# Linear attention into a snake MLP on one core: the first MLP group moved ahead of the second group's attention

## The chip, the cores and the metric

The kernel runs on one core of a Trainium2 chip, in one launch. The metric is the device time of a run in microseconds. The core's engines work side by side and wait for each other by semaphores: TensorE (PE, and PEld for its weight loads), VectorE (DVE), ScalarE (ACT), GpSimd (POOL) and SyncE (SP), which here issues transfers only.

## The reference

A causal linear attention with a decay per head, in blocks of 64, is followed by an MLP. Batch 4, 8 heads, 768 positions, head size 64; then 3072 tokens by 512 features, with 2048 hidden features.

```python
for b in range(nb):                       # blocks of 64 positions
    intra = einsum('bhic,bhjc->bhij', qb, kb) * Dmask      # lam**(i-j), causal
    intra = einsum('bhij,bhjd->bhid', intra, vb)
    inter = einsum('bhid,bhde->bhie', qb * lam_pow, kv_state)
    out[:, :, sl] = intra + inter
    kv_state = lam_block * kv_state + einsum('bhsd,bhse->bhde', kb * rev_pow, vb)
x = out.transpose(0, 2, 1, 3).reshape(B * S, H * D)
h = x @ w_in
s = sin(alpha * h)
g = h + s * s / (alpha + 1e-09)
y = g @ w_out
```

## The kernel before, in words

The work is cut into 24 units, `u` = 0 to 23. A unit is one batch, four heads and 256 positions, in two chunks of 128. Four units make a group of 512 tokens, so there are 6 groups, and the MLP runs by groups. The main loop walks through slots, `n` = 0 to 32.

**Loads.** `load(u)` (L68) issues the q, k and v of a unit, 256 KB each, on SyncE's queue, into a ring of 10 stage buffers. Before the loop the first 10 units are issued at once; in slot n unit n + 10 follows. The weights w_in and w_out come in four chunks each on GpSimd's queue (L135, L141), changed from fp32 to bf16 on the way.

**Scaling.** `scale(u)` (L149) makes three bf16 tiles: QL (q times a power of lam), KD (k divided by it) and VB (v). In the first group QL is made on VectorE and VB on ScalarE, otherwise all three on GpSimd. It is called two slots ahead.

**A slot of attention.** `transposes(u)` (L173) turns QL and KD on TensorE into one PSUM tile, pt, and ScalarE copies it to QT. `scores(u)` (L196) multiplies them into sp, which uses the same PSUM buffer as pt, and VectorE writes the masked ST from it. `kvmm(u)` (L218) makes the k-v products of the unit in the PSUM tile okv, and `kvupd(u)` (L233) updates the state: kvx on VectorE, kvbd and kvs on GpSimd, for each chunk. One slot later `intermm` (L261) and `outmm` (L275) put the attention output of the unit into okv (there is one okv, made anew for each slot), and `outev` (L291) has ScalarE copy it to xt. `slot(n)` (L302) puts these in order.

**The MLP.** `ffn1(g, f)` (L314) is one of 16 hidden blocks: four matmuls into hps (three PSUM buffers), Sin on ScalarE to s1, the square s2 on VectorE, and gall = s2 * r + hps on VectorE. `ffn2(g, m)` (L338) is one of four row blocks of the second layer: 16 matmuls into ops (one PSUM buffer), a copy to ob on ScalarE and a store on SyncE's queue.

**Order.** In slot n, four hidden blocks of group (n - 4) // 4 run between four blocks of four second-layer matmuls of group (n - 8) // 4; the transposes of the next unit stand behind the first of these (L390 to L395). So the first layer of group 0 runs in slots 4 to 7, beside the attention of group 1. TensorE's order is the written one (`manual_schedule`, L363). On the other engines a planner orders the instructions by its own priorities.

Of the kernel before, what the change touches and what calls it, by code (L numbers as in the profile page):

```python
# [9 lines left out]
ALU = mybir.AluOpType  # L10
ACTF = mybir.ActivationFunctionType
FP32 = mybir.dt.float32
BF16 = mybir.dt.bfloat16
PE = mybir.EngineType.PE


@with_exitstack
def kernel(
# [15 lines left out]
    C = 128  # L34
# [32 lines left out]

    def load(u):  # L68
        _, tp, b, _, hh = where(u)
        st = []  # L70
        for nm, src in (("q", q), ("k", k), ("v", v)):
            tl = stagep.tile([P, HH, 2, D], FP32, name=f"st_{nm}")
            nc.sync.dma_start(  # L73
                out=tl[:].rearrange("p h two e -> p h (two e)"),
                in_=src[b, hh * HH:(hh + 1) * HH, tp * W:(tp + 1) * W, :]
                .rearrange("h (p two) e -> p h (two e)", two=2))
            st.append(tl)
        stage[u] = st

    lam_bc = consts.tile([P, H], FP32, name="lam_bc")  # L80
    nc.sync.dma_start(out=lam_bc[:], in_=lam.partition_broadcast(P))
    alpha_r = consts.tile([NFC, P], FP32, name="alpha_r")
    nc.scalar.dma_start(out=alpha_r[:], in_=moe_alpha.rearrange("(f p) -> f p", p=P))
    for u in range(RING):
        load(u)
# [4 lines left out]
    for c in range(2):  # L90
# [11 lines left out]
    make_identity(nc, idf[:])  # L102
    cT = consts.tile([P, 1], FP32, name="cT")
    nc.vector.memset(cT[:], float(C))
    mask = consts.tile([P, 2, 2 * D], BF16, name="mask")
# [13 lines left out]
    lam_v = lam_bc[:].rearrange("p (hp two) -> p two hp", two=2)

    def make_lhp():
        for hd in range(2):
            sl = slice(hd * D, (hd + 1) * D)
            nc.gpsimd.tensor_tensor(out=LHP[sl, :], in0=lam_v[sl, hd, :],
                                    in1=cT[sl, :].to_broadcast([D, HP]), op=ALU.pow)
            nc.vector.tensor_copy(out=LBD[sl, :, hd], in_=LHP[sl, :])

# [173 lines left out]

    def slot(n, okv):  # L302
        if n < NU:
            scores(n)
        if 1 <= n <= NU:
            outmm(n - 1, okv)
            outev(n - 1, okv)
        if n < NU:
            kvmm(n, okv)
            kvupd(n, okv)  # L310

    gall = {}

    def ffn1(g, f):  # L314
        if f == 0:
# [3 lines left out]
        for c in range(NDC):  # L319
            def step(c=c):  # L320
                nc.tensor.matmul(out=hps[:], lhsT=w_in_sb[:, c, f * P:(f + 1) * P],  # L321
                                 rhs=xt[g][:, c].rearrange("p b c i -> p (b c i)"),
                                 start=(c == 0), stop=(c == NDC - 1))
            steps.append(step)

        def fin():
            s1 = mlps.tile([P, 512], BF16, name="s1")
            nc.scalar.activation(out=s1[:], in_=hps[:], func=ACTF.Sin,  # L328
                                 scale=alpha_sb[:, f:f + 1])
            s2 = mlps.tile([P, 512], BF16, name="s2")  # L330
            nc.vector.tensor_tensor(out=s2[:], in0=s1[:], in1=s1[:], op=ALU.mult)  # L331
            nc.vector.scalar_tensor_tensor(out=gall[g][:, f, :], in0=s2[:],  # L332
                                           scalar=r_sb[:, f:f + 1], in1=hps[:],
                                           op0=ALU.mult, op1=ALU.add)
# [26 lines left out]

    NM = NU + 8
    with tc.manual_schedule(engines={PE}):  # L363
        scale(0)
        run(transposes(0))
        scale(1)
        make_lhp()
        load_w_in(0)
        ap = ps.tile([P, NFC], FP32, name="ap", tag="ops", bufs=1)
        nc.tensor.transpose(out=ap[:], in_=alpha_r[:], identity=idf[:])  # L370
        nc.vector.tensor_copy(out=alpha_sb[:], in_=ap[:])
        nc.vector.reciprocal(out=r_sb[:], in_=alpha_sb[:])
        for n in range(NM + 1):
            g1, g2 = (n - 4) // 4, (n - 8) // 4
            A2 = A1 = None
            if n <= NU:
                slot(n, intermm(n - 1) if n >= 1 else new_okv())
            if n + 2 < NU:
                scale(n + 2)
            if n + RING < NU:  # L380
                load(n + RING)
            if n < 3:
                load_w_in(n + 1)
            elif n < 7:
                load_w_out(n - 3)
            T_ = transposes(n + 1) if n + 1 < NU else []
            A2 = ffn2(g2, n % 4) if 0 <= g2 < NG else []
            A1 = ([ffn1(g1, (n % 4) * 4 + i) for i in range(4)] if 0 <= g1 < NG
                  else [[] for i in range(4)])
            for i in range(4):  # L390
                run(A2[4 * i:4 * i + 4])
                if i == 0:
                    run(T_)
                run(A1[i])
            run(A2[16:])  # L395

# [29 lines left out]
```

## Time and profile before

| | us |
|---|---|
| median of 2 runs (lowest to highest) | 296.72 (296.6 to 296.84) |
| profiled run: time | 296.46 |
| profiled run: span from first to last instruction | 294.7 |
| TensorE busy in the span | 219.9 (75%) |
| VectorE busy | 157.9 (54%) |
| ScalarE busy | 121.6 (41%) |
| GpSimd busy | 106.9 (36%) |

The page's slices of the span, 40 of equal length (busy tenths of each engine, the granted TensorE clock in tenths, the DMA engines' busy share and what they moved), are read from left to right:

```profile
PE   0314518578578998899889988998899999999820
DVE  1812313866776666666666556655675666662000
POOL 6839957544654346434643344131000000000000
PEclk9999999987999999999999999999999999999995
DMA  7999999999943321000100010001000101111111
GB/s 189 261 267 253 237 215 272 287 290 291 290 122 78 103 68 35 19 26 31 36 23 24 31 38 21 24 30 38 20 24 29 38 28 35 41 39 39 51 51 39
```

A row of the timeline below gives the start, the duration, the engine and line, what is written from what, and in brackets how long the engine stood idle before it and what ended that. The lines of the chain in order of time give start, duration and the work. A matmul's duration is modelled and overlaps its neighbours, so the pace of matmuls is read from their starts or from the chain.

### The profile page before, as it was taken

What the parts mean: (1) busy time and instruction counts of PE and PEld (TensorE: products, weight loads), DVE (VectorE), ACT (ScalarE), POOL (GpSimd) and SP (SyncE); (2) the same over time, 40 slices, a digit from 0 to 9 for tenths busy, and PEclk for the clock granted to TensorE, in tenths of its full rate; (3) what the DMA queues carried; (4) which work ended last, traced back from release to release, by engine and by line L of the source; (5) the groups of instructions that cost most, each with busy time, mean ns of one, the idle gap of its engine ahead of it and who ended that gap; (6) DMA issues with size and microseconds to landing.
All of it is one profiled execution on the core that took longest, in us unless ns stands there. A gap on an engine that the chain in (4) does not pass through costs nothing.

```text
span 294.7 us, 5308 instructions
## 1 busy us (share of the span) xinstructions
PE 219.9 (75%) x2129; PEld 112.4 (38%) x2129; DVE 157.9 (54%) x293; ACT 121.6 (41%) x174; POOL 106.9 (36%) x160
## 2 busy tenths in 40 slices
PE   0314518578578998899889988998899999999820
PEld 0213414334244444444444444444444444444300
DVE  1812313866776666666666556655675666662000
ACT  2222214355444644454445444544454345451100
POOL 6839957544654346434643344131000000000000
PEclk9999999987999999999999999999999999999995
DMA  7999999999943321000100010001000101111111
GB/s 189 261 267 253 237 215 272 287 290 291 290 122 78 103 68 35 19 26 31 36 23 24 31 38 21 24 30 38 20 24 29 38 28 35 41 39 39 51 51 39
DMA packets 45560, 29.71 MB, mean 101 GB/s; under 512 B 1488, under 2 KB 42464, under 8 KB 45536
## 3 DMA queue, kind: packets, MB, share of 16 engines
q1 hardware_dynamic: 41280, 25.17, 31.2%
q0 software_dynamic: 4224, 4.19, 8.4%
q8 instruction: 16, 0.26, 0.4%
q14 instruction: 8, 0.07, 0.1%
q10 hardware_dynamic: 32, 0.01, 0.0%
HBM read 27.28 MB, written 6.29 MB: 114 GB/s over the span
## 4 chain that ended last, share of the span: by engine, by line
PE 55%; DVE 15%; SPq 8%; ACT 6%; DMA 5%; issue 5%; POOL 1%; ACTq 0%; POOLq 0%
PE hps L321 26%; PE ops L343 24%; SPq L73 8%; DVE ST L210 7%; DMA st_k<-in_k_dram 5%; PE pt L182 4%; DVE gall L332 4%; ACT ob L350 1%; ACT L328 0%; ACT xt L295 0%; PE okv L284 0%; DVE s_670 L331 0%; PE sp L203 0%; PE okv L268 0%; DVE s_1066 L331 0%
## 5 line engine op out<-in xcount | busy, mean ns | idle before, releaser
L321 PE MATMUL hps<-xt,w_in_sb 128*128 128x512 bf16 x384 | 101.5, 393 | 1.5 <-DVE gall L332 1.5
L343 PE MATMUL ops<-w_out_sb,gall 128*128 128x512 bf16 x384 | 96.7, 379 | 2.1 <-ACT ob L350 2.1
L321 PEld LDWEIGHTS <-w_in_sb 128*128 128x128 bf16 x384 | 38.0, 101 | 46.1 <-issue 8.1
L343 PEld LDWEIGHTS <-gall 128*128 128x128 bf16 x384 | 36.2, 98 | 44.6 <-issue 2.9
L188 ACT COPY QT<-pt 128x1024 bf16<-128x1024 bf16 x24 | 24.3, 1012 | 50.6 <-PE pt L182 50.6
L210 DVE TENSOR_TENSOR ST<-sp,mask 128x512 bf16<-128x512 f32 x48 | 32.4, 684 | 4.6 <-PE sp L203 4.6
L161 POOL TENSOR_TENSOR KD<-st_k,R 128x512 bf16<-128x512 f32 x24 | 24.9, 1040 | 16.5 <-DMA st_k<-in_k_dram 12.2
L182 PE MATMUL pt<-iden,QL 128*128 128x128 bf16 x96 | 10.8, 244 | 21.9 <-DVE ST L210 12.4
L168 POOL CAST VB<-st_v 128x512 bf16<-128x512 f32 x20 | 14.2, 711 | 33.8 <-PE okv L284 33.6
L295 ACT CAST xt<-okv 128x512 bf16<-128x512 f32 x24 | 14.1, 586 | 20.2 <-PE okv L284 18.4
L350 ACT COPY ob<-ops 128x512 f32<-128x512 f32 x24 | 14.1, 586 | 17.4 <-PE ops L343 17.4
L158 POOL TENSOR_TENSOR QL<-st_q,E 128x512 bf16<-128x512 f32 x20 | 20.8, 1042 | 0.0
L227 PE MATMUL okv<-VB,KD 64*64 64x64 bf16 x320 | 8.1, 207 | 15.8 <-ACT xt L295 15.8
L182 PEld LDWEIGHTS <-QL 128*128 128x128 bf16 x96 | 6.2, 106 | 29.9 <-DVE ST L210 20.2
L227 PEld LDWEIGHTS <-KD 64*64 64x64 bf16 x320 | 8.1, 118 | 18.7 <-issue 18.7
L203 PE MATMUL sp<-QT 64*64 64x128 bf16 x384 | 11.1, 241 | 2.0 <-ACT QT L188 2.0
L182 PE MATMUL pt<-iden,KD 128*128 128x128 bf16 x96 | 11.0, 246 | 0.6 <-POOL KD L161 0.6
L284 PE MATMUL okv<-ST,VB 64*64 64x128 bf16 x384 | 10.4, 232 | 0.0
L203 PEld LDWEIGHTS <-QT 64*64 64x64 bf16 x384 | 6.9, 116 | 4.9 <-ACT QT L188 2.1
L182 PEld LDWEIGHTS <-KD 128*128 128x128 bf16 x96 | 7.7, 112 | 0.8 <-POOL KD L161 0.8
L284 PEld LDWEIGHTS <-VB 64*64 64x64 bf16 x384 | 7.7, 118 | 0.1
L166 ACT CAST VB<-st_v 128x512 bf16<-128x512 f32 x4 | 2.5, 618 | 11.8 <-DMA st_v<-in_v_dram 11.8
(501 smaller groups left out, 273.2 us busy)
## 6 DMA issues: line engine op xcount, KB each, us to landing
st_q<-in_q_dram SPq DMA_DIRECT2D x24, 256.0 KB
st_k<-in_k_dram SPq DMA_DIRECT2D x24, 256.0 KB
st_v<-in_v_dram SPq DMA_DIRECT2D x24, 256.0 KB
out_dram<-ob SPq DMA_DIRECT2D x24, 256.0 KB
w_in_sb<-in_moe_w_in_dram POOLq DMA_DIRECT2D x4, 512.0 KB, 8.7
w_out_sb<-in_moe_w_out_dram POOLq DMA_DIRECT2D x4, 512.0 KB, 10.6
alpha_r<-in_moe_alpha_dram ACTq DMA_DIRECT2D x1, 8.0 KB
lam_bc<-in_lam_dram SPq DMA_DIRECT2D x1, 4.0 KB
```

Of the source, the lines that this page charges most:

```text
L73: nc.sync.dma_start(out=tl[:].rearrange("p h two e -> p h (two e)"), in_=src[b, hh * HH:(hh + 1) * HH, tp * W:(tp + 1) * W, :] .rearrange( ...
L158: eq.tensor_tensor(out=QL[:], in0=qs[:].rearrange("p h two e -> p two h e"), in1=E[:, :, hs].unsqueeze(3).to_broadcast([P, 2, HH, D]), op= ...
L161: nc.gpsimd.tensor_tensor(out=KD[:], in0=ks[:].rearrange("p h two e -> p two h e"), in1=R[:, :, hs].unsqueeze(3).to_broadcast([P, 2, HH, D ...
L182: nc.tensor.transpose(out=pt[:, j, hp, par, :], in_=src[:, par, 2 * hp:2 * hp + 2, :], identity=iden[:])
L188: nc.scalar.copy(out=QT[:], in_=pt[:])
L203: nc.tensor.matmul(out=sp[half[c], hd, par, hp, :], lhsT=QT[half[hd], 1, hp, par, half[c]], rhs=QT[half[hd], 0, hp, :, half[c]], start=Tru ...
L210: nc.vector.tensor_tensor(out=ST[:, hd], in0=sp[:, hd], in1=mask[:].unsqueeze(2).to_broadcast([P, 2, 2, P]), op=ALU.mult)
L227: nc.tensor.matmul(out=okv[half[hd], c, 2 * P + hp * D:2 * P + (hp + 1) * D], lhsT=KD[half[c], par, h, :], rhs=VB[half[c], par, h, :], sta ...
L284: nc.tensor.matmul(out=okv[half[hd], c, hp * P:(hp + 1) * P], lhsT=VB[half[c], par, 2 * hp + hd, :], rhs=ST[half[c], hd, par, hp, :], star ...
L321: nc.tensor.matmul(out=hps[:], lhsT=w_in_sb[:, c, f * P:(f + 1) * P], rhs=xt[g][:, c].rearrange("p b c i -> p (b c i)"), start=(c == 0), s ...
L343: nc.tensor.matmul(out=ops[:], lhsT=gall[g][:, f, m * P:(m + 1) * P], rhs=w_out_sb[:, f, :], start=(f == 0), stop=(f == NFC - 1))
L350: nc.scalar.copy(out=ob[:], in_=ops[:])
```

## The change

- Before the loop only units 0 to 3 are loaded. The load of unit 4, and with it the loads behind it on SyncE's queue (up to unit 13), waits for the last matmul of hidden block f = 9 of group 0.
- Slots 0 to 3 hold the attention of group 0 alone. Then all 16 hidden blocks of group 0 run in a row, with the square of the odd ones on GpSimd, and after them the scaling and the transposes of unit 4.
- In slots 4 to 6 the attention of group 1 runs beside second-layer row blocks 0 to 2 of group 0; slot 7 has no MLP work; row block 3 is spread over slots 8 to 11, beside the first layer of group 1. From slot 12 on the groups are as before.
- In a slot, the transposes of the next unit stand in the third round of MLP blocks instead of the first.
- In `slot`, kvmm comes ahead of the copy of okv to xt (outev).
- The order of GpSimd and SyncE is the written one too.
- w_in is issued in slots 0 and 1, two chunks each, behind the state update and the scaling; w_out after slot 3.
- lam to the power of 128 is made by repeated multiplication on VectorE instead of a power on GpSimd. A Sin of one element stands at the start of ScalarE's work.

```diff
+    GATE = 9
-    def load(u):
+    def load(u, after=None):
...
-            nc.sync.dma_start(
+            ld = nc.sync.dma_start(
...
+            if after is not None:
+                tc.add_manual_dep(ld.ins, after.ins.name, mybir.DependencyInfo(
+                    mybir.DependencyClass.Sync, mybir.DependencyReason.DATA))
+                after = None
...
+    nc.scalar.activation(out=warm[:], in_=warm[:], func=ACTF.Sin)
...
-    for u in range(RING):
+    for u in range(4):
         load(u)
...
+    LT = consts.tile([P, H], FP32, name="LT")
+    nc.vector.tensor_tensor(out=LT[:], in0=lam_bc[:], in1=lam_bc[:], op=ALU.mult)
+    for i in range(6):
+        nc.vector.tensor_tensor(out=LT[:], in0=LT[:], in1=LT[:], op=ALU.mult)
...
-    def slot(n, okv):
+    def slot(n):
+        okv = intermm(n - 1) if 1 <= n <= NU else new_okv()
         if n < NU:
             scores(n)
         if 1 <= n <= NU:
             outmm(n - 1, okv)
+        if n < NU:
+            kvmm(n, okv)
+        if 1 <= n <= NU:
             outev(n - 1, okv)
         if n < NU:
-            kvmm(n, okv)
             kvupd(n, okv)
...
-            nc.vector.tensor_tensor(out=s2[:], in0=s1[:], in1=s1[:], op=ALU.mult)
+            (sq or nc.vector).tensor_tensor(out=s2[:], in0=s1[:], in1=s1[:], op=ALU.mult)
...
+    def blocks(steps, k):
+
+        n = (len(steps) - 1) // k
+        bl = [steps[i * n:(i + 1) * n] for i in range(k)]
+        bl[-1] = bl[-1] + steps[-1:]
+        return bl
+
-    NM = NU + 8
-    with tc.manual_schedule(engines={PE}):
+    with tc.manual_schedule(engines={ET.PE, ET.Pool, ET.SP}):
         scale(0)
+        scale(1)
         run(transposes(0))
-        scale(1)
-        make_lhp()
-        load_w_in(0)
...
+        for n in range(4):
+            slot(n)
+            if n + 2 < 4:
                 scale(n + 2)
+            if n < 2:
+                load_w_in(2 * n)
+                load_w_in(2 * n + 1)
             if n < 3:
+                run(transposes(n + 1))
+        for j in range(4):
+            load_w_out(j)
+        okv = intermm(3)
+        outmm(3, okv)
+        outev(3, okv)
+        for f in range(NFC):
+            run(ffn1(0, f, nc.gpsimd if f % 2 else nc.vector))
+            if f == GATE:
+                load(4, after=f1mm[0, f])
+                for u in range(5, 4 + RING):
+                    load(u)
+        scale(4)
+        scale(5)
+        run(transposes(4))
+        NM = NU + 4
+        for n in range(4, NM):
+            if n < NU:
+                if n == 4:
+                    okv = new_okv()
+                    scores(4)
+                    kvmm(4, okv)
+                    kvupd(4, okv)
+                else:
+                    slot(n)
+                if n + 2 < NU:
+                    scale(n + 2)
+                if n + RING < NU:
+                    load(n + RING)
+            elif n == NU:
+                slot(n)
+            i = n % 4
+            g = n // 4
             T_ = transposes(n + 1) if n + 1 < NU else []
...
+            F1 = [ffn1(g - 1, 4 * i + j) for j in range(4)] if g >= 2 else []
+            if g == 1:
+                F2 = blocks(ffn2(0, i), 4) if i < 3 else []
+            elif g == 2:
                 if i == 0:
+                    late = blocks(ffn2(0, 3), 4)
+                F2 = [late[i]]
+            else:
+                F2 = blocks(ffn2(g - 2, i), 4)
+            nb = max(len(F1), len(F2), 3)
+            for j in range(nb):
+                if j < len(F2):
+                    run(F2[j])
+                if j == 2:
+                    run(T_)
+                if j < len(F1):
+                    run(F1[j])
+        for i in range(4):
+            run(ffn2(NG - 1, i))
```

## Rows read from the trace of the kernel before

**Rows 1.** Stretches: start and end, length, engines' busy time, granted clock, DMA.

```profile
0.00:48.10 48.10, 14.15 (x281) 10.99 (x282) 15.37 (x32) 10.96 (x14) 33.89 (x56) 1.00 1.12 239
48.10:81.22 33.12, 23.87 (x240) 11.55 (x239) 21.97 (x41) 17.30 (x23) 18.11 (x27) 0.90 1.11 290
81.22:236.92 155.70, 139.14 (x1400) 70.65 (x1398) 100.23 (x187) 76.48 (x111) 54.93 (x77) 1.00 0.13 40
236.92:281.80 44.88, 42.76 (x213) 19.18 (x211) 20.35 (x35) 16.29 (x25) 0.00 (x0) 1.00 0.12 40
```

**Rows 2.** The chain that ended last, shares of the span by line.

```profile
PE hps L321 26%; PE ops L343 24%; SPq L73 8%; DVE ST L210 7%; DMA st_k<-in_k_dram 5%; PE pt L182 4%; DVE gall L332 4%; ACT ob L350 1%; ACT L328 0%; ACT xt L295 0%; PE okv L284 0%; DVE s_670 L331 0%; PE sp L203 0%; PE okv L268 0%; DVE s_1066 L331 0%
```

**Rows 3.** Timeline of the startup, 0 to 50 us.

```profile
1.20 0.41 SPq L73 DMA_DIRECT2D st_q<-in_q_dram  x1
...
6.49 0.62 ACT L166 CAST VB<-st_v 128x512 bf16<-128x512 f32 x1 [4.03 <-DMA st_v<-in_v_dram]
...
7.60 0.95 POOL L137 DMA_DIRECT2D w_in_sb<-in_moe_w_in_dram  x1
...
13.49 0.64 PE L203 MATMUL sp<-QT 64*64 64x128 bf16 x16 [2.02 <-ACT QT L188]
...
15.39 0.28 DVE L245 COPY kvx<-okv 128x128 f32<-128x128 f32 x1
...
21.59 1.03 POOL L161 TENSOR_TENSOR KD<-st_k,R 128x512 bf16<-128x512 f32 x1 [3.66 <-DMA st_k<-in_k_dram]
...
24.03 0.37 PE L268 MATMUL okv<-QT,kvbd_256 128*128 128x128 bf16 x2 [7.47 <-DVE kvx L247]
...
29.07 0.37 PE L268 MATMUL okv<-QT,kvbd_349 128*128 128x128 bf16 x2 [1.58 <-DVE kvx L247]
...
48.10 4.27 PE L321 MATMUL hps<-xt,w_in_sb 128*128 128x512 bf16 x12
```

**Rows 4.** Timeline of a steady slot.

```profile
110.98 0.22 PE L268 MATMUL okv<-QT,kvbd_447 128*128 128x128 bf16 x1
...
112.62 0.32 PE L227 MATMUL okv<-VB,KD 64*64 64x64 bf16 x16 [0.69 <-ACT xt L295]
...
114.24 0.40 PE L182 MATMUL pt<-iden,QL 128*128 128x128 bf16 x4 [0.33 <-DVE ST L210]
...
120.74 0.22 PE L268 MATMUL okv<-QT,kvbd_539 128*128 128x128 bf16 x1
```

**Rows 5.** The chain in order of time: four MLP matmuls, start and duration.

```profile
115.72 0.86 PE ops L343 x4
```

**Rows 6.** Transfers by line: KB of each, median us from issue to landing.

```profile
w_in_sb<-in_moe_w_in_dram POOLq DMA_DIRECT2D x4, 512.0 KB, 8.7
```

**Rows 7.** Timeline of slots 4 to 7.

```profile
50.73 0.69 ACT L328 ACTIVATE s_668<-hps,alpha_sb 128x512 bf16<-128x512 f32 x1
...
51.45 0.92 DVE L331 TENSOR_TENSOR s_670<-s_668 128x512 bf16<-128x512 bf16 x1
...
52.40 0.75 DVE L332 SCALAR_TENSOR_TENSOR gall<-s_670,r_sb,hps 128x512 bf16<-128x512 bf16 x1
...
53.07 0.42 DVE L331 TENSOR_TENSOR s_679<-s_677 128x512 bf16<-128x512 bf16 x1
...
58.49 5.06 PE L321 MATMUL hps<-xt,w_in_sb 128*128 128x512 bf16 x16
...
72.75 0.28 PE L268 MATMUL okv<-QT,kvbd_891 128*128 128x128 bf16 x2
...
76.48 0.40 PE L182 MATMUL pt<-iden,QL 128*128 128x128 bf16 x4 [1.88 <-DVE ST L210]
...
81.22 0.28 PE L268 MATMUL okv<-QT,kvbd_1023 128*128 128x128 bf16 x2
```

**Rows 8.** Groups of instructions on GpSimd: count, busy us and mean ns, idle before.

```profile
L161 POOL TENSOR_TENSOR KD<-st_k,R 128x512 bf16<-128x512 f32 x24 | 24.9, 1040 | 16.5 <-DMA st_k<-in_k_dram 12.2 <-PE okv L227 3.4 <-POOL VB L168 0.9
```

**Rows 9.** Line 158 on VectorE: duration in ns, least, median and most.

```profile
L158 DVE TENSOR_TENSOR QL<-st_q,E x4: 628/678/3042, 8.1 to 13.1; 128x512 bf16<-128x512 f32 x4
```

More of the change, by code (lines that the diff above doesn't have):

```diff
@@ L13 @@
 BF16 = mybir.dt.bfloat16
-PE = mybir.EngineType.PE
+ET = mybir.EngineType
 @with_exitstack
@@ L76, in load @@
                 .rearrange("h (p two) e -> p h (two e)", two=2))
+            if after is not None:
+                tc.add_manual_dep(ld.ins, after.ins.name, mybir.DependencyInfo(
+                    mybir.DependencyClass.Sync, mybir.DependencyReason.DATA))
+                after = None
             st.append(tl)
         stage[u] = st
+    warm = consts.tile([1, 1], FP32, name="warm")
+    nc.vector.memset(warm[:], 0.0)
+    nc.scalar.activation(out=warm[:], in_=warm[:], func=ACTF.Sin)
     lam_bc = consts.tile([P, H], FP32, name="lam_bc")
@@ L102 @@
     make_identity(nc, idf[:])
-    cT = consts.tile([P, 1], FP32, name="cT")
-    nc.vector.memset(cT[:], float(C))
     mask = consts.tile([P, 2, 2 * D], BF16, name="mask")
@@ L118 @@
     nc.vector.memset(LBD[:], 0.0)
[L119 to L126, printed above, removed]
+    LT_v = LT[:].rearrange("p (hp two) -> p two hp", two=2)
+    for hd in range(2):
+        sl = slice(hd * D, (hd + 1) * D)
+        nc.vector.tensor_copy(out=LHP[sl, :], in_=LT_v[sl, hd, :])
+        nc.vector.tensor_copy(out=LBD[sl, :, hd], in_=LT_v[sl, hd, :])
     alpha_sb = consts.tile([P, NFC], FP32, name="alpha_sb")
@@ L306, in slot, with ffn1 @@
             outmm(n - 1, okv)
+        if n < NU:
+            kvmm(n, okv)
+        if 1 <= n <= NU:
             outev(n - 1, okv)
         if n < NU:
-            kvmm(n, okv)
             kvupd(n, okv)
     gall = {}
-    def ffn1(g, f):
+    f1mm = {}
+    def ffn1(g, f, sq=None):
         if f == 0:
@@ L320, in step @@
             def step(c=c):
-                nc.tensor.matmul(out=hps[:], lhsT=w_in_sb[:, c, f * P:(f + 1) * P],
+                f1mm[g, f] = nc.tensor.matmul(out=hps[:], lhsT=w_in_sb[:, c, f * P:(f + 1) * P],
                                  rhs=xt[g][:, c].rearrange("p b c i -> p (b c i)"),
@@ L372 @@
         nc.vector.reciprocal(out=r_sb[:], in_=alpha_sb[:])
[L373 to L378, printed above, removed]
+        for n in range(4):
+            slot(n)
+            if n + 2 < 4:
                 scale(n + 2)
-            if n + RING < NU:
-                load(n + RING)
+            if n < 2:
+                load_w_in(2 * n)
+                load_w_in(2 * n + 1)
@@ L382 @@
             if n < 3:
-                load_w_in(n + 1)
-            elif n < 7:
-                load_w_out(n - 3)
-            T_ = transposes(n + 1) if n + 1 < NU else []
[L387 to L391, printed above, removed]
-                if i == 0:
+                run(transposes(n + 1))
@@ L393 @@
                     run(T_)
-                run(A1[i])
-            run(A2[16:])
+                if j < len(F1):
+                    run(F1[j])
+        for i in range(4):
+            run(ffn2(NG - 1, i))
 _INS = ['q', 'k', 'v', 'lam', 'moe_w_in', 'moe_w_out', 'moe_alpha']
```

## The prediction, made before the changed kernel ran

> **What bounds the kernel now.** I read the stretches first, then the chain of waits, then the timeline inside each stretch. The stretches [rows 1] fall into four parts. In the first 48.10 us TensorE is busy for 14.15 us only, while the DMA engines are saturated at 239 GB/s and GpSimd is busy for 33.89 us. [...] From 81.22 to 236.92 (slots 8 to 23) it works 139.14 of 155.70 us at 1.00. From 236.92 to the end of the span, 57.8 us, it is busy 42.76 of 44.88 us and then leaves the last store to run out. The chain of waits [rows 2] agrees: MLP matmuls are half of the span, and of the rest the largest pieces are the load queue (8%), ST on VectorE (7%) and a k load (5%).
>
> The startup [rows 3] shows how loads get into the attention chain. Slot 0's scores run at 13.49 and its kvx is made by 15.39, but GpSimd, whose order a planner wrote, stands in front of a KD whose k tile has not landed (3.66 us of waiting, KD at 21.59). The state update of slot 0 is behind it, so slot 1 begins at 24.03 after 7.47 us of idle TensorE. Where no load is late, a slot takes 29.07 - 24.03 = 5.04 us. The first MLP matmul comes at 48.10.
>
> In the steady part [rows 4] a slot is 120.74 - 110.98 = 9.76 us. Four MLP matmuls take 0.86 us [rows 5], so the 32 of a slot take 6.91. Two idle times of TensorE are left: kvmm waits 0.69 us for the copy of xt, and the transposes wait 0.33 us for ST, whose PSUM buffer they share. So 9.76 - 6.91 - 0.69 - 0.33 = 1.83 us are attention's own matmuls.
>
> The profiled run's span of 294.7 lies 1.76 us under its time of 296.46, and the median is 0.26 above that time. I sum on the span and add 2.0.
>
> **Startup to the first MLP matmul: 30.2 instead of 48.10.** Only units 0 to 3 are loaded and GpSimd follows program order, so the KD of unit 4 no longer stands before slot 0's state update. Ahead of the first transposes GpSimd loses two LHP powers and one w_in issue (0.95 us, at 7.60 [rows 3]); the eight small LT multiplies that replace the powers go to VectorE, beside GpSimd's power for E. I take slot 0's scores at 11 (bounds 10 and the old 13.5). kvx comes 1.9 us later, as now; GpSimd's two products and the second kvx bring slot 1 to 11 + 3.7 = 14.7. Slots 1 and 2 take 5.04 each, slot 3 about 4 since no weight issue lies in it, and the last intermm, outmm and copy of xt 1.5 (an estimate from the 1.83 of all attention matmuls and a copy of about 0.6): 30.2. The two w_in issues now lie behind slot 0's update and the KD of unit 2, near 16.7 instead of 7.60, and the last two near 22. With 8.7 us from issue to landing [rows 6] the first two chunks are in near 26; the last two, for which the queue must bring 2 MB more, near 33. The first is needed at 30.2, the third at 41: hidden. The four w_out issues sit on GpSimd behind slot 3 (about 3 us, to 33), ahead of the first square there at 34; their 4 MB, read at the 290 GB/s of the second stretch [rows 1], land near 49 and are needed at 58. The Sin table load moves to the start, where ScalarE waits for data.
>
> **The first MLP group alone: 20.2 us.** [...] I take two f at 2 x 0.86 = 1.73 us each, 3.4 in all, then 14 limited by the three hps buffers. A buffer is filled (0.86), read by Sin (0.69), squared, and freed by gall (0.75) [rows 7]. With 0.3 of handing over (an estimate), an even f takes 0.86 + 0.69 + 0.42 + 0.75 + 0.3 = 3.0 us. An odd f has its square on GpSimd, which no row shows; the nearest row is KD, a 128x512 product too, at 1.04 [rows 8], giving 3.6. Over three buffers that is 1.1 us per f. VectorE's products of two SBUF tiles also vary while GpSimd is at work: QL took 0.63 us at best and 3.04 at worst [rows 9], and a square 0.92 instead of 0.42 [rows 7]. Half of one such delay per pair, 0.25, makes it 1.2. Bounds: 0.96 (VectorE's (0.42 + 0.75 + 0.75)/2) and 1.7 (the lower clock throughout). 3.4 + 14 x 1.2 = 20.2, so the group ends at 50.4.
>
> **The gate and the restart: 6.0 us of TensorE idle.** SyncE's load of unit 4 waits for the matmul of f = 9, at 30.2 + 3.4 + 8 x 1.2 = 43.2. Behind it on that queue are 29 more loads, and later the first stores, which nobody needs before slot 7. Unit 0's q, k and v were in 5.3 us after the first issue (from 1.20 to the cast at 6.49 [rows 3]); the same here gives 48.5. GpSimd, in order, has the square of f = 15 first, until 52.4, so the load is hidden; if w_out's packets double the 5.3, it is 53.8 and costs 1.4. Then QL and KD (2 x 1.04), transposes and the QT copy follow: scores of slot 4 at 56.4.
>
> **Slots 4 to 7: 22.6 us.** Slot 4 has 1.2 us of attention, 16 second-layer matmuls of which I put eight at the lower clock (3.45 + 1.73), and 0.46 of transposes: 6.9. Slots 5 and 6 have 3.45 + 1.83 = 5.3 of TensorE work, just over the 5.04 of a slot that GpSimd paces; slot 7 has no MLP: 5.04 less a weight issue, 4.3. With 0.8 for a colder start of slot 8 this is 22.6, and slot 8 begins at 79.0; now it begins at 81.22 [rows 7].
>
> **Slots 8 to 23: 133.1 instead of 155.7.** In slots 8 to 11 the work falls to 20 MLP matmuls, since three quarters of the second layer are done. TensorE then needs 4.32 + 1.83 = 6.15, and VectorE, whose work in a slot stays as it is, 100.23 / 16 = 6.3 [rows 1]. Today's slot 7, the same work less four matmuls, takes 81.22 - 72.75 = 8.5, with a 1.88 us wait of the transposes for ST in it [rows 7] and the 0.69 for xt; both go, since the transposes get two more blocks in front of them. 8.5 - 1.88 - 0.69 + 0.86 = 6.8; I take 7.2 for the slots in which VectorE's order gets in the way, 28.8 in all. In slots 12 to 22 both idle times go: kvmm stands before the copy, and the transposes behind five blocks (4.3 us) where now one block and 0.33 us are enough for ST. That is 11 x (9.76 - 1.02) = 96.1. Slot 23 has no transposes: 8.2. What is late next: QT's copy (1.01) has three blocks, 2.6 us, until the next scores; and kvx now stands behind the copy of xt in their PSUM bank, some 0.7 later, with 4 us to spare.
>
> **End: 57.8,** unchanged. Sum: 79.0 + 133.1 + 57.8 = 269.9, and 272 as a time.
>
> **Rivals.** *Cold start-up (8%).* TensorE stays at the lower clock until slot 8. For it: the granted clock was 0.90 between 48.10 and 81.22, where TensorE idled up to 1.88 us at a time, and 16 matmuls took 5.06 us [rows 1, 7]. Against: 0.90 is the mean of a stretch in which it rose again each time. All 16 f at 1.73 add 7.5, and slots 4 to 6 at 9.3 (16 x 0.43 + 2.4 of attention) add 10.4: 290. [...]
>
> *The wait changes place (10%).* The 0.69 us come back as a wait for kvx or the copy: 15 x 0.69 = 10.4 more, 282. [...]
>
> *Less in the way (17%).* The lone group at 0.96 per f (-3.4), slots 8 to 11 at TensorE's 6.15 (-4.2), no cold slot 8 (-0.8): 263.5. For it: VectorE was busy only 100.23 of 155.70 us [rows 1].
>
> *Planner's order stays (5%).* VectorE and ScalarE are still ordered by the planner, so the change does only part of what it says: if ST and kvx wait behind gall and the squares as in today's slot 7, slots 4 to 7 and 8 to 11 last 8.5 each at most, 34.0 instead of 22.6 for the first four, where VectorE has little else to do in three of them, so I count half of that, and 5.2 more for the others: 283.
>
> *Slower (3%).* The transposes moved so late that QT is not ready for the next scores. Place: slots 5 to 22, 18 of them. A slot loses whatever the copy exceeds 2.6 us; the change loses more than 2% from 1.7 us per slot on (30.8/18), that is, if the copy is done 4.3 us after the transposes. At 1.9 per slot it is 306. ScalarE, busy 76.48 of 155.70 us [rows 1], speaks against it.
>
> **How the numbers follow.** My sum has 57%, with its own range of 266 to 279 from the bounds (first scores +2.5/-1, the lone group -3.4/+7, w_out +1.4, slots 8 to 11 -4/+5, taken together rather than added). The range of 263 to 285 takes in 263.5 and 282, and leaves out the cold start and the slower case, 11%, and a little of the tails. A measurement here can tell about 2% from no change: under 290.8 is faster, over 302.7 slower. Faster: 57 + 10 + 17 + 5 and half of the cold case, 93%. The other half is no change, 4%. Slower 3%.
>
> **What would show it.** First MLP matmul near 30, a pace of 1.2 us per f and a longer idle time before slot 4's scores near 56; slot 8 near 79; slots of 7.2 and then 8.7 us, with no idle time before kvmm and the transposes. I am wrong if slot 8 starts past 95, if an idle time before scores names the QT copy, or if kvmm's 0.69 shows up under another name.

## The result, and the profile after

The changed kernel takes 268.25 us (median of 2 runs, 267.57 to 268.93) against 296.72: a ratio of 0.904 (95% interval 0.8941 to 0.914). The forecast was 272.0 with a range of 263 to 285, and faster. The profiled run took 267.57 us with a span of 265.8.

The first view is the table of stretches, cut where the prediction's steps end (start and end, length, each engine's busy time with its instructions, granted clock, DMA share, GB/s); it answers to [rows 1].

```profile
0.00:32.83 32.83, 11.15 (x234) 8.42 (x236) 13.17 (x38) 9.94 (x14) 18.85 (x39) 1.00 0.79 161
32.83:52.07 19.24, 16.27 (x62) 6.22 (x62) 12.53 (x21) 10.61 (x16) 9.86 (x11) 1.00 1.00 192
52.07:57.73 5.66, 1.22 (x9) 0.69 (x9) 2.38 (x4) 1.70 (x2) 4.80 (x6) 0.76 1.22 292
57.73:78.00 20.27, 17.41 (x259) 9.95 (x263) 7.11 (x16) 7.13 (x10) 15.86 (x26) 0.90 1.17 286
78.00:107.94 29.94, 24.69 (x315) 13.18 (x320) 21.63 (x44) 16.48 (x25) 18.29 (x28) 0.94 0.66 190
107.94:200.07 92.13, 91.45 (x947) 49.00 (x957) 73.19 (x128) 53.16 (x77) 44.24 (x58) 1.00 0.17 54
...
```

The first number of a line after its length is TensorE's busy time. From 107.94 on it works 91.45 of 92.13 us: nothing is left to wait for in slots 12 to 22. What is idle lies before that: most in the startup, then in slots 8 to 11 (24.69 of 29.94), the restart (52.07 to 57.73), the lone group (the first MLP group's first layer, which now runs by itself, 16.27 of 19.24) and slots 4 to 7 (17.41 of 20.27). Three of these stretches have a granted clock below 1.00. It is at its lower level, 0.50 in the profile, from 55.02 to about 61.9, in the restart and slot 4, and again from about 79 to 82, in slot 8.

A steady slot, in the timeline of TensorE, answers to [rows 4]:

```profile
116.31 0.22 PE L276 MATMUL okv<-QT,kvbd_805 128*128 128x128 bf16 x1
...
116.88 0.39 PE L292 MATMUL okv<-ST,VB 64*64 64x128 bf16 x16
117.10 0.29 PE L235 MATMUL okv<-VB,KD 64*64 64x64 bf16 x16
...
121.66 0.39 PE L190 MATMUL pt<-iden,QL 128*128 128x128 bf16 x4
...
124.69 0.22 PE L276 MATMUL okv<-QT,kvbd_917 128*128 128x128 bf16 x1
```

124.69 - 116.31 is 8.38 us, against 9.76. No row has an idle time in brackets: kvmm (L235) follows outmm (L292) after 0.22 us, and the transposes (L190) come behind five blocks.

The startup, in the timeline of all engines, answers to [rows 3]:

```profile
12.34 0.62 ACT L174 CAST VB<-st_v 128x512 bf16<-128x512 f32 x1 [2.10 <-DMA st_v<-in_v_dram]
...
13.92 0.64 PE L211 MATMUL sp<-QT 64*64 64x128 bf16 x16 [4.79 <-ACT QT L196]
...
17.62 0.37 PE L276 MATMUL okv<-QT,kvbd_228 128*128 128x128 bf16 x2 [0.62 <-DVE kvx L255]
```

Slot 1 begins at 17.62 instead of 24.03. But the scores of slot 0, at 13.92, are no earlier than before (13.49): ScalarE stands for 2.10 us in front of a cast whose v tile has not landed, and QT's copy, at 12.86, is behind it.

The restart, in the timelines of GpSimd (first two rows) and TensorE, answers to [rows 7, 8]:

```profile
52.92 1.04 POOL L344 TENSOR_TENSOR s_734<-s_732 128x512 bf16<-128x512 bf16 x1 [1.09 <-ACT s_732 L341]
53.92 1.04 POOL L166 TENSOR_TENSOR QL<-st_q,E 128x512 bf16<-128x512 f32 x1
...
55.02 0.61 PE L190 MATMUL pt<-iden,QL 128*128 128x128 bf16 x4 [2.95 <-POOL QL L166]
...
57.73 0.64 PE L211 MATMUL sp<-QT 64*64 64x128 bf16 x16 [1.10 <-ACT QT L196]
```

GpSimd makes the last square of the lone group first and then QL of unit 4, for which TensorE has stood since 52.07.

### The profile page after: what moved, and what is told of

The parts are those of the page before. It is cut to its first block, busy times and chain, and to the rows that moved or that the text cites. A ratio compares the mean times of both kernels' runs of the same rounds, so it can differ in the third digit from the quotient of the medians.

```text
span 265.8 us, 5296 instructions
## 1 busy us (share of the span) xinstructions
PE 212.6 (80%) x2104; PEld 110.6 (42%) x2129; DVE 156.7 (59%) x294; ACT 119.8 (45%) x174; POOL 112.5 (42%) x166
## 4 chain that ended last, share of the span: by engine, by line
PE 63%; POOL 13%; issue 6%; DVE 5%; ACT 4%; SPq 2%; DMA 2%; POOLq 0%; ACTq 0%
PE ops L356 30%; PE hps L334 24%; PE sp L211 3%; POOL KD L169 3%; PE pt L190 3%; POOL QL L166 2%; DMA st_v<-in_v_dram 2%; DVE gall L345 2%; SPq L74 2%; ACT QT L196 2%; PE okv L292 2%; PE okv L276 1%; POOL w_in_sb L145 1%; DVE ST L218 1%; DVE kvx L255 1%
## 5 line engine op out<-in xcount | busy, mean ns | idle before, releaser
L334 PE MATMUL hps<-xt,w_in_sb 128*128 128x512 bf16 x381 | 98.6, 384 | 7.8 <-DVE gall L345 6.8
L334 PEld LDWEIGHTS <-w_in_sb 128*128 128x128 bf16 x384 | 37.3, 99 | 53.3 <-issue 14.8
L166 POOL TENSOR_TENSOR QL<-st_q,E 128x512 bf16<-128x512 f32 x20 | 22.4, 1122 | 0.0
L190 PE MATMUL pt<-iden,QL 128*128 128x128 bf16 x96 | 10.4, 238 | 14.2 <-DVE QL L166 7.4
L190 PEld LDWEIGHTS <-QL 128*128 128x128 bf16 x96 | 7.3, 104 | 19.8 <-DVE QL L166 7.4
L176 POOL CAST VB<-st_v 128x512 bf16<-128x512 f32 x20 | 13.1, 656 | 0.0
L190 PE MATMUL pt<-iden,KD 128*128 128x128 bf16 x96 | 10.5, 239 | 0.7 <-POOL KD L169 0.7
L292 PE MATMUL okv<-ST,VB 64*64 64x128 bf16 x384 | 10.5, 232 | 0.0
L235 PE MATMUL okv<-VB,KD 64*64 64x64 bf16 x320 | 7.7, 205 | 0.0
L292 PEld LDWEIGHTS <-VB 64*64 64x64 bf16 x384 | 7.6, 117 | 0.3 <-issue 0.2
L190 PEld LDWEIGHTS <-KD 128*128 128x128 bf16 x96 | 7.1, 107 | 1.2 <-POOL KD L169 1.2
L235 PEld LDWEIGHTS <-KD 64*64 64x64 bf16 x320 | 6.4, 122 | 0.0
```

The lines of the kernel that those rows point to most:

```text
L166: eq.tensor_tensor(out=QL[:], in0=qs[:].rearrange("p h two e -> p two h e"), in1=E[:, :, hs].unsqueeze(3).to_broadcast([P, 2, HH, D]), op= ...
L190: nc.tensor.transpose(out=pt[:, j, hp, par, :], in_=src[:, par, 2 * hp:2 * hp + 2, :], identity=iden[:])
L235: nc.tensor.matmul(out=okv[half[hd], c, 2 * P + hp * D:2 * P + (hp + 1) * D], lhsT=KD[half[c], par, h, :], rhs=VB[half[c], par, h, :], sta ...
L292: nc.tensor.matmul(out=okv[half[hd], c, hp * P:(hp + 1) * P], lhsT=VB[half[c], par, 2 * hp + hd, :], rhs=ST[half[c], hd, par, hp, :], star ...
L334: f1mm[g, f] = nc.tensor.matmul(out=hps[:], lhsT=w_in_sb[:, c, f * P:(f + 1) * P], rhs=xt[g][:, c].rearrange("p b c i -> p (b c i)"), star ...
```

## The experiments

Each was timed in three rounds beside the kernel before; ratios are to that kernel, with their 95% interval. "After" is the changed kernel.

### The two edits in a slot

**One edit undone: the copy of xt again ahead of kvmm.**

```diff
+        if 1 <= n <= NU:
+            outev(n - 1, okv)
         if n < NU:
             kvmm(n, okv)
-        if 1 <= n <= NU:
-            outev(n - 1, okv)
```

> The changed kernel (268.25) with one thing undone: in a slot the copy of okv to xt stands ahead of kvmm again. Theory A, idle time read from starts: before the change kvmm began 1.09 us behind the first outmm matmul, after it 0.22, so the wait is worth 0.87 a slot. In the 12 slots 12 to 23, which TensorE paces, that is 10.4 us more, with up to 5 on top in slots 5 to 11: 279 to 284. Theory B, the idle time as printed (0.69): 8.3 more, 276 to 277. Theory C, the wait only changed its place: no more than 270.

Measured: 283.3 us (279.48 to 284.05), 0.957 (0.9554 to 0.9586). Timeline of TensorE, a steady slot:

```profile
118.29 0.39 PE L276 MATMUL okv<-QT,kvbd 128*128 128x128 bf16 x4
...
118.86 0.39 PE L292 MATMUL okv<-ST,VB 64*64 64x128 bf16 x16
119.94 0.32 PE L235 MATMUL okv<-VB,KD 64*64 64x64 bf16 x16 [0.69 <-ACT xt L303]
...
127.55 0.39 PE L276 MATMUL okv<-QT,kvbd 128*128 128x128 bf16 x4
```

The slot is 9.26 us. The bracket says 0.69, as in [rows 4], but kvmm begins 119.94 - 118.86 = 1.08 us behind outmm where after has 0.22: the wait is worth 0.86, and the slot is longer by 0.88. The printed idle time counts from the modelled end of the 16 small matmuls (118.86 + 0.39 = 119.25) and leaves a part out. The trace is of the quickest run, 279.48, and it accounts for that run: 1.1 us before slot 12 and 0.88 in each of slots 12 to 23 make up the 11.6 us by which its span is longer than that of after (277.4 and 265.8). The other runs took some 3 to 4 us more and have no trace, so where they lost that is not shown.

**The other edit undone: the transposes again behind the first block.**

```diff
-                if j == 2:
+                if j == 0:
                     run(T_)
```

> The changed kernel with one thing undone: the transposes of the next unit stand in the first round of MLP blocks again. Theory A: ST is ready 2.9 us after the scores begin, whatever TensorE does, so with kvmm early the transposes wait longer by just what kvmm gained: slots 12 to 22 go back to 9.76 us, 11 x 1.38 = 15 more, and some in slots 4 to 11: 283 to 288. Rival: the two edits add up, and this one is worth only its own 0.5 a slot, 5.5 more: 274.

Measured: 288.02 us, 0.9718 (0.9703 to 0.9732). Timeline of TensorE, a steady slot:

```profile
121.56 0.39 PE L276 MATMUL okv<-QT,kvbd 128*128 128x128 bf16 x4
121.88 0.42 PE L211 MATMUL sp<-QT 64*64 64x128 bf16 x16
...
122.58 1.04 PE L356 MATMUL ops<-w_out_sb,gall 128*128 128x512 bf16 x4
124.91 0.38 PE L190 MATMUL pt<-iden,QL 128*128 128x128 bf16 x4 [1.30 <-DVE ST L218]
...
131.50 0.39 PE L276 MATMUL okv<-QT,kvbd 128*128 128x128 bf16 x4
```

9.94 us: with the transposes early, what the earlier kvmm saves comes back in front of them, as 1.30 us for ST where [rows 4] has 0.33. ST is ready no earlier: the transposes begin 3.03 us after the scores here (121.88, 124.91) and 2.94 us in a slot of the kernel before (121.06, 124.00):

```profile
121.06 0.42 PE L203 MATMUL sp<-QT 64*64 64x128 bf16 x16
121.30 0.39 PE L284 MATMUL okv<-ST,VB 64*64 64x128 bf16 x16
122.39 0.32 PE L227 MATMUL okv<-VB,KD 64*64 64x64 bf16 x16 [0.69 <-ACT xt L295]
122.64 1.04 PE L343 MATMUL ops<-w_out_sb,gall 128*128 128x512 bf16 x4
124.00 0.40 PE L182 MATMUL pt<-iden,QL 128*128 128x128 bf16 x4 [0.33 <-DVE ST L210]
```

TensorE only reaches the wait sooner.

**Both undone.**

> The changed kernel with both orders within a slot undone, so that the new startup, the lone group and the in-order GpSimd and SyncE are left. Theory A: slots 12 to 22 at 9.76 us, 15 to 20 more than 268.25, and within 3 us of the run with the transposes alone undone: 283 to 289. Rival (the edits add up): the sum of the two increments.

Measured: 291.25 us, 0.9828 (0.9812 to 0.9844), a little above what was expected. This is the new startup alone: some 5 us, less than the 2% that can be told from no change here. The steady slots are those of the run before it, 9.94 us in slots 13 to 16 and 9.84 from slot 17 on, in both runs. So in a steady slot kvmm alone gives nothing, the later transposes alone about 0.6 (9.84 to 9.26) and both together 1.46 (to 8.38). The edits do not add: the time that the first saves in front of kvmm is lost in front of the transposes until the second moves these. Slot 23 shows it from the other side. It has no transposes, and there the earlier kvmm pays by itself: 8.81 us in this run, 7.93 in the one before. The rest of the 3.2 us between the two runs lies mostly in slot 8 (9.79 and 7.52), where TensorE was at about half pace in this run (the first four second-layer matmuls take 1.89 us, at 82.69) and not in the other (1.04, at 80.59).

**The two edits alone, in the kernel before.** There kvmm moves ahead of the copy and the transposes behind the fifth block:

```diff
             outmm(n - 1, okv)
-            outev(n - 1, okv)
         if n < NU:
             kvmm(n, okv)
+        if 1 <= n <= NU:
+            outev(n - 1, okv)
+        if n < NU:
             kvupd(n, okv)
...
-                if i == 0:
+                if i == 2:
                     run(T_)
```

> The kernel before (296.72) with only the two orders within a slot changed: kvmm ahead of the copy to xt, transposes behind the third block of second-layer matmuls. Theory A: slots 8 to 22 at 8.38 instead of 9.76 take off 20.8, slot 23 0.9, slots 4 to 7 another 4 to 8: 267 to 271, that is as fast as the whole change. Rival: the startup, the lone group and the orders of GpSimd and SyncE bring a third or more of the gain, and this run stays above 276.

Measured: 267.85 us (266.09 to 268.5), 0.9028 (0.8993 to 0.9062): as fast as the whole change. Two of its stretches, slot 4 and slots 8 to 11, and a row of its timeline in slot 4:

```profile
40.54:53.81 13.27, 7.18 (x74) 3.62 (x75) 4.56 (x10) 5.10 (x7) 7.81 (x12) 0.88 1.13 258
...
74.47:107.87 33.40, 33.40 (x368) 17.71 (x366) 25.65 (x50) 19.35 (x28) 19.72 (x28) 1.00 0.55 144
```

```profile
52.15 1.86 PE L323 MATMUL hps<-xt,w_in_sb 128*128 128x512 bf16 x4 [6.00 <-DVE gall L334]
```

Slot 12 begins at 107.87, in the changed kernel at 107.94, with the same work done. So the rearranged startup, as it stands, is worth nothing beside the slot edits: its first MLP matmul comes 9.4 us earlier (32.83, here 42.22), and it gives that back in the restart and in slots 8 to 11, which here run without any idle time (33.40 of 33.40). Nor is the old startup at its best. The 6.00 us of waiting in slot 4 are the fault of [rows 3] once more: in the chain of waits a k load ends at 48.55, and behind it follow on GpSimd the KD that it feeds (48.69), kvbd and kvs, and on VectorE kvx (50.69), a square and the gall that TensorE waits for.

### The parts of the new startup

**No gate:** the load of unit 4 no longer waits for f = 9 (`load(4, after=f1mm[0, f])` becomes `load(4)`).

> The changed kernel without the gate: the loads of units 4 to 13 follow those of unit 3 at once. Theory A: the gate costs nothing (GpSimd came to unit 4's scaling only when its last square was done, at 53.92) and protects little, since the w_in chunks are needed 10 us after they land: 267 to 270. Rival, the purpose of the gate: the loads delay w_in by half of its 6.6 us to landing or more, and the first MLP matmul comes 4 us or more later: 272 or more.

Measured: 267.87 us, 0.9046 (0.9021 to 0.907), no different from after. The median landing of a w_in chunk went from 6.6 to 10.9 us and of w_out from 8.9 to 14.4, but slot 12 begins at 107.98. Holding the loads back does what it says to the transfers and nothing that the time shows. The trace has a small effect under it: slot 5 begins 1.0 us later than in after (65.06 and 64.05), and slot 8 is 1.0 us shorter (6.74 and 7.73), since TensorE was at half clock there in after (0.50 from about 79 to 82) and at full pace here: the slot's second-layer matmuls, of which the traces have three, take 1.49 us in after and 0.81 here.

**GpSimd in the planner's order** (`engines={ET.PE, ET.SP}`).

> The changed kernel with GpSimd ordered by the planner again. It puts the KDs of units 2 and 3 ahead of slot 0's state update, w_in earlier, and unit 4's scaling among the squares of the lone group. Theory A (my prediction's step): a KD ahead of the state update makes the first slots wait for loads, the startup loses 2 us or more, and a square waits behind the scaling for unit 4's load: 270 to 274. Rival: with four units loaded first no load is late any more, so the order does not matter: 267 to 269.

Measured: 273.53 us, 0.924 (0.9214 to 0.9267). Scores of slot 0 move to 16.25, QL of unit 4 goes between the squares, at 49.75, and yet slot 8 begins at 80.91 and slot 12 at 112.83. The written order on GpSimd is worth some 5 us.

**ScalarE in written order too** (`ET.Activation` added).

> The changed kernel with ScalarE in written order too; it differs in the startup alone, where the first QT copy no longer stands behind the cast of unit 2's v. Theory A: in the changed kernel scores of slot 0 came at 13.92 and not at 11 because that copy waited for this load; in order it runs behind unit 1's cast (9.62 + 0.62), scores at 11.3, and the 2.6 us carry through the startup: 265 to 266.5. Rival: weights or loads are next in line, and nothing is left of it by slot 4: 268.

Measured: 266.76 us, 0.9025 (0.8986 to 0.9063), just above the expected range. The scores of slot 0 come at 11.04, the predicted 11, but of these 2.9 us slot 1 keeps 0.9 (16.69 against 17.62). A row of TensorE's timeline says why:

```profile
15.03 0.61 PE L190 MATMUL pt<-iden,QL 128*128 128x128 bf16 x4 [3.13 <-DVE ST L218]
```

Now VectorE, still planned, stands with ST behind unit 3's QL, which begins at 13.08 after 1.65 us of waiting for its load. The same fault, one engine on. By slot 5 nothing is left of the 0.9 (64.10 against 64.05), as the rival had it. Slot 12 is 0.9 earlier (107.03) only because slot 8, at full pace (0.81 us for the same three), takes 6.74 us here, against 7.73 in after, where the clock was at 0.50 for some 3 us of it.

**VectorE and ScalarE in written order** (`ET.DVE` as well).

> The changed kernel with VectorE and ScalarE in written order too. With ScalarE alone in order, scores of slot 0 came at 11.04, but VectorE stood in front of unit 3's QL, whose load was late, and ST came 2 us later. Theory A: both engines in order remove both waits; slot 1 begins at 14.7 instead of 17.62, as my sum had it, and the 2.9 us last to the end: 264.5 to 266. Rival: w_in or the loads of units 2 and 3 are next, and no more than the 1.5 us of ScalarE alone is left: 266.5 to 268.

Measured: 266.09 us, 0.8986 (0.8957 to 0.9014), between the two ranges. Slot 1 begins at 14.94 (predicted 14.7), 2.7 us earlier than in after, and the first MLP matmul at 30.92 (30.2), 1.9 earlier. At slot 8 1.4 us are left (76.59). Slot 12 is 2.4 us earlier (105.54), but 1.0 of that is slot 8, which ran at half clock in after (0.50) and at full pace here (6.74 us, and 0.81 for the same three matmuls). So about half of the gain lasts. Slots 9 to 11 still take 7.40 us each: the planner's order on VectorE was not what held them.

### The lone MLP group and the restart

**All squares on VectorE:** `run(ffn1(0, f, nc.gpsimd if f % 2 else nc.vector))` becomes `run(ffn1(0, f))`.

> The changed kernel with all squares of the lone group on VectorE. Theory A: the group then runs at VectorE's pace, 0.42 + 0.75 = 1.17 us per f, hardly slower than the 19.65 us that it takes now, and GpSimd is free to scale unit 4 as soon as its loads land, near 50, instead of 53.92, so scores of slot 4 come 2 to 4 us earlier: 264 to 267. Rival: eight squares more on VectorE cost 3.4 us, and the load is no earlier: 270 to 272.

Measured: 260.8 us (260.07 to 262.77), 0.8819 (0.8772 to 0.8867), better than expected. The timeline of all engines, 48 to 59 us:

```profile
48.07 1.04 POOL L166 TENSOR_TENSOR QL<-st_q,E 128x512 bf16<-128x512 f32 x1 [12.97 <-DMA st_q<-in_q_dram]
48.16 1.23 DVE L344 TENSOR_TENSOR s<-s 128x512 bf16<-128x512 bf16 x1
...
54.11 0.42 PE L211 MATMUL sp<-QT 64*64 64x128 bf16 x16 [1.23 <-ACT QT L196]
```

The lone group itself is no faster (its last matmul ends at 52.27, against 52.07). But GpSimd, free, makes QL of unit 4 as soon as its load is there, 48.07 instead of 53.92, so slot 4's scores come 3.6 us earlier. Slot 5 comes 5.6 earlier (58.49, and 64.05 in after). The other 2 us are the clock: from 57.73 to about 61.9 TensorE works at half pace, which makes 2.1 us of work out of 4.2. Two tables of stretches, first of after, then of this kernel (granted clock third from the right):

```profile
55.00:56.00 1.00, 0.61 (x4) 0.34 (x4) 0.00 (x0) 0.00 (x0) 1.00 (x2) 0.51 1.22 290
...
60.00:62.00 2.00, 2.00 (x6) 0.71 (x5) 0.29 (x1) 0.00 (x0) 1.59 (x4) 0.54 1.22 290
```

```profile
52.00:54.00 2.00, 0.88 (x10) 0.53 (x8) 1.97 (x4) 1.53 (x2) 2.00 (x3) 1.00 1.17 302
54.00:56.00 2.00, 1.84 (x38) 1.13 (x40) 1.96 (x5) 0.06 (x1) 0.52 (x1) 1.00 1.20 289
```

In after TensorE stands from 52.07 to 55.02, and restarts at a clock of 0.51; it is back at 1.00 by 62 (62 to 64), and six matmuls take the 2 us from 60. Here, with idle times of 1.23 us at most, it stays at 1.00. Slot 8 adds 1.0 us: 7.73 in after, at half clock (0.50) from about 79 to 82, and 6.74 here. That last microsecond can't be put down to the restart, since without the gate or with ScalarE in order the restart is at half pace too (0.64 us for slot 4's 16 score matmuls, 0.42 here) and slot 8 takes 6.74 all the same.

**Squares on GpSimd for odd f below 8 only** (`... if f % 2 and f < 8 else nc.vector`), to part the restart from the pace of the group.

> The changed kernel with the odd squares on GpSimd for f below 8 alone, so half of them on GpSimd and the late ones on VectorE. It tells what made all squares on VectorE 7.4 us faster. Theory A: the restart. [...] Rival: the pace of the lone group, in which eight squares of 1.04 us on GpSimd stand between hps and gall: half of the gain, 264 to 265.

Measured: 262.25 us, 0.8847 (0.8825 to 0.887): 6.0 of the 7.4 us, more than the rival's half, though half of the GpSimd squares are left. What costs is GpSimd being busy when unit 4 lands, and what follows from it, rather than its slower square. TensorE is at full pace in slot 4, behind a wait of 1.24 us (0.42 us for the 16 score matmuls, at 54.45), and at half pace in slot 8 from 73 to about 76.5 (0.64 us for the same, at 73.00; the clock's mean from 58 to 78 is 0.91), behind waits of 1.14 and 0.97 us in slot 7. The kernel with all squares on VectorE has the same two waits in slot 7, and there slot 8 is at full pace (0.42, at 72.65; the clock is 1.00 from 58 to 78). What decides this is not shown.

### Going further

**Squares on VectorE, and kvs ahead of kvbd on GpSimd:** the second chunk's kvx needs kvs alone, so the product that makes kvs is issued before the one for kvbd.

```diff
             bd = kvp.tile(...)
-            nc.gpsimd.tensor_tensor(out=bd[:], ...)
             ...
                 nc.gpsimd.tensor_tensor(out=prev[:], ...)
+            nc.gpsimd.tensor_tensor(out=bd[:], ...)
```

> All squares on VectorE (260.8), and in the state update kvs is made ahead of kvbd on GpSimd. Theory A: in slots 8 to 11 TensorE waits 1.40 us for gall because VectorE, in its order, stands in front of the second kvx, which waits for kvs behind kvbd; with kvs 0.6 us earlier each of these slots is 0.6 shorter, and each of the first slots 0.3 (kvbd is then the last to come): 256.5 to 259. Rival: VectorE's work sets these slots, the wait only moves to another square: 260 to 261.

Measured: 257.38 us (256.77 to 258.6), 0.8697 (0.8664 to 0.8729), the best of all. The total was expected, the place was not: slots 9 to 11 still take 7.40 us each, as in after. One of them in TensorE's timeline:

```profile
79.35 0.38 PE L190 MATMUL pt<-iden,QL 128*128 128x128 bf16 x4 [0.54 <-DVE ST L218]
...
81.57 1.02 PE L334 MATMUL hps<-xt,w_in_sb 128*128 128x512 bf16 x4 [0.75 <-DVE gall L345]
```

The 1.40 us wait for gall of after has split in two, both for VectorE. VectorE is now at work for 20.33 of the 22.19 us of these three slots (17.80 of 22.21 in after): there the rival was right. Against the kernel with all squares on VectorE (260.8), 1.6 us are gained in the startup, 1.7 between the first MLP matmul and the scores of slot 4, and 0.4 each in slots 4 to 7 and in slot 8 (6.33).

**All together:** the last, VectorE and ScalarE in written order, and the last group's second-layer tiles in the three hps buffers instead of the single ops buffer, so that TensorE need not wait for the copies to ob.

```diff
+        if g == NG - 1 and m > 0:
+            ops = ps.tile([P, DM], FP32, name="ops2", tag="hps", bufs=3)
+        else:
+            ops = ps.tile([P, DM], FP32, name="ops", tag="ops", bufs=1)
```

> All squares on VectorE, kvs ahead of kvbd, VectorE and ScalarE in written order, and the last three row blocks of the second layer in the hps buffers, which are free by then, so that they need not wait 0.67 us each for the copy of the one before. If the parts add up: 260.8 - 3.5 - 2.9 - 2.0 = 252.4. Range 251 to 256. Rival: with the startup shorter the loads of unit 4 are the next to wait for, and half of the 2.9 and 3.5 is lost: 256 to 258.

Measured: 258.64 us (257.66 to 259.04), 0.8721 (0.8693 to 0.8749): outside both ranges, and no faster than without the additions. The written order starts the lone group 1.12 us earlier (29.75 against 30.87), but slot 4's scores come at 50.81 against 50.77. The chain of waits has it: the first seven matmuls take 3.21 us against 2.83, and a square of the lone group, on VectorE beside GpSimd's work on unit 4, takes 1.05 instead of 0.35. Slots 9 to 11 take 0.1 us longer each. At the end it is the stores. In the timelines, first of this kernel, then of the one without the additions:

```profile
225.94 15.23 SPq L369 DMA_DIRECT2D out_dram<-ob  x5
...
240.05 0.59 ACT L366 COPY ob<-ops 128x512 f32<-128x512 f32 x1 [2.87 <-PE ops L359]
```

```profile
225.53 17.77 SPq L366 DMA_DIRECT2D out_dram<-ob  x5
...
242.18 0.59 ACT L363 COPY ob<-ops 128x512 f32<-128x512 f32 x1 [3.75 <-PE ops L356]
```

The last copy is 2.1 us earlier, but the span ends at 255.4 here and at 255.0 there, in both 29.5 us after the fifth store from the end was issued. The stretches of this kernel show what fills them:

```profile
235.00:240.00 5.00, 4.97 (x24) 2.04 (x21) 0.00 (x0) 0.59 (x1) 0.00 (x0) 1.00 0.13 51
240.00:245.00 5.00, 0.00 (x0) 0.00 (x0) 0.00 (x0) 0.59 (x1) 0.00 (x0) 1.00 0.13 52
```

The stores move 51 to 52 GB/s, before and after TensorE has stopped, at a DMA share of 0.13: about two of the 16 engines. A store of 262,144 bytes then takes 5.1 us, and TensorE made one each 4.33 us already. So the end hangs on the stores, and a faster TensorE only lengthens their queue. That the store's layout is what keeps it to that share was not tried.

## Why the prediction was right, and where its steps were off

| step | predicted | measured |
|---|---|---|
| to the first MLP matmul | 30.2 | 32.83 |
| lone group | 20.2 | 19.24 |
| restart, to the scores of slot 4 | 6.0 | 5.66 |
| slots 4 to 7 | 22.6 | 20.27 |
| slots 8 to 11 | 28.8 | 29.94 |
| slots 12 to 22 | 96.1 | 92.13 |
| slot 23 | 8.2 | 7.93 |
| end | 57.8 | 57.8 |
| span | 269.9 | 265.8 |

The steps come in the order and for most of the reasons that the prediction gave; their sizes are off, and the errors (measured less predicted) partly cancel: +2.6, -1.0, -0.3, -2.3, +1.1, -4.0, -0.3.

**The largest error is the steady slot, 8.74 predicted and 8.38 measured.** The step that was mis-sized is "both idle times go", which I priced as printed, 0.69 + 0.33 = 1.02. Measured by starts, in the rows of the kernel before shown with the second experiment, kvmm began 122.39 - 121.30 = 1.09 us behind outmm, and 0.22 in after: 0.87. The transposes began 124.00 - 122.64 = 1.36 us after the block whose four matmuls take 0.86 [rows 5]: 0.50. Together 1.37, against 9.76 - 8.38 = 1.38. The first experiment confirms the 0.87. The first three together show that the wait before kvmm pays only once the transposes are moved, while moving the transposes alone gives some 0.6 a slot.

**The startup** missed its own 11 for slot 0's scores, and the bounds of 10 to 13.5 with it (13.92): it left out that the planner still orders ScalarE and VectorE, which the rival on the planner's order placed in slots 4 to 11. With both in written order slot 1 begins at 14.94 and the group at 30.92. The remaining steps of 5, 5 and 4 us were right in the changed kernel (5.02, 4.84, 4.07).

**The lone group** was right within 1 us; its first eleven matmuls take 3.40 us in the chain, 1.0 more than at full pace (I put 1.7 on that). The sum's two f at half pace are what the kernel before shows, where the first eight matmuls, from 48.10 on, begin 0.43 us apart and the next 0.22; in the changed kernel only the first five in the trace do. The square on GpSimd takes the estimated 1.04. **The restart** was right within 0.4 us, but the prediction counted it as given. It is a cost of the square of f = 15 standing on GpSimd ahead of QL: without GpSimd's squares slot 5 comes 5.6 us earlier. The w_out and gate terms were rightly nothing, the gate within the 1 us named above.

**Slots 4 to 7** were 2.3 us shorter than my sum, although the clock was low (0.50) until about 62 and some eight second-layer matmuls of slot 4 (58.52 to 61.88) ran at that level, as in the sum; 0.8 of that is the colder start that I put there for slot 8. It did come, in slot 8 itself, and took 1.0. **Slots 8 to 11** have the wait of which I took a part. TensorE's timeline has three rows like this one:

```profile
92.27 1.02 PE L334 MATMUL hps<-xt,w_in_sb 128*128 128x512 bf16 x4 [1.40 <-DVE gall L345]
```

**The end** came out at 57.8 as in the kernel before, but for a reason that I did not give: stores set it, not TensorE. From 240 to 260 us they moved 50 to 52 GB/s in the changed kernel too.

Of the rivals, *the wait changes place* fails in the changed kernel (no idle time in a steady slot) and appears in the second experiment. *Cold start-up* is true in the startup, by the pace of its matmuls (0.64 us for 16 score matmuls, 0.42 from slot 5 on), and after it from 55 to 62 us and from 79 to 82 only (0.50). The trace has a start at half clock after 2.95 us without a matmul (0.51), and none after the waits of up to 0.95 us inside the lone group (1.00). *Planner's order stays* is true in slot 0, at 2.7 us, of which about half lasts; in slots 8 to 11, where it was placed, it is not. One of my signs of being wrong, an idle time before scores that names QT's copy, did occur, in slot 0 (4.79) and slot 4 (1.10). The sign as written does not say in which slots; in the steady ones it does not occur.

**Where the expected gain went.** My sum reached slot 8 only 2.2 us sooner than the kernel before and left most of the gain to the slots behind it; that part is right, and the runs go further: with the slot edits alone in the kernel before, slot 12 comes at the same time. Here the right total is in part luck. In my sum the slot edits are worth 15 x 1.02 + 0.69, some 16 of 24.8 us, and the new order of the work the other 9. By themselves the slot edits gave 28.4 us, and beside them the new order gave nothing. The first MLP matmul is 15.3 us earlier (32.83 for 48.10), and TensorE's waits in the lone group, the restart and slots 8 to 11 use that up: 3.0, 4.4 and 5.3 us idle in the stretches above, and some 10 us at half pace. With GpSimd free at the restart the new startup is worth 6 to 7 us (260.8 against 267.85; by the ratios 0.8819 against 0.9028). Whether the old one could be mended as far was not tried.

## What to carry to other kernels

Size a wait by the starts of the instructions around it, not by the printed idle time, and ask what the engine meets next if it arrives earlier: of two waits in one loop, the first may pay only once the second is moved too. When work is moved ahead of a load, the engine that must process that load (here GpSimd) should not be given the tail of the moved work. Before speeding up the last stage, divide the output by the rate of its stores.

## What the runs showed of the hardware

- The same bf16 square of 128x512 takes 1.04 us on GpSimd and 0.42 on VectorE.
- VectorE's square takes 1.23 us when it begins 0.09 us after GpSimd's QL (48.16 and 48.07 above). It ends 0.28 us after QL, where it takes 0.42 by itself.
- After 2.95 us without a matmul TensorE restarted at a clock of 0.51 and had 1.00 again some 7 us later, with TensorE busy for all of the last 2 us. After waits of 1.14 and about 0.97 us in slot 7 it fell to half pace in slot 8 in two kernels (after, at a clock of 0.50, and the one with odd squares below 8 on GpSimd) and stayed at full pace in others with the same waits (1.00 with all squares on VectorE).
- In the first 32.83 us of after the clock column shows 1.00, yet the 16 score matmuls take 0.64 us there, as at 57.73, where it shows 0.50; from slot 5 on they take 0.42. There the pace tells the level, and the column does not.
- Stores of 256 KB drained at 51 to 52 GB/s, a DMA share of 0.13, whatever TensorE did; while loads ran, 302 GB/s were moved (52 to 54 us, all squares on VectorE).
